# A planner that sets the order of every instruction: transfers booked as one queue of at most eight, hand-over times by pair of engines, and one store for each converted piece

## The chip, the cores and the metric

One core of a Trainium2 chip runs the whole program. The metric is device time in microseconds (us) of one execution. Engines are named as in the profile: PE (matmuls; PEld its weight loads), DVE (VectorE), ACT (ScalarE), POOL (GpSimd) and SP (SyncE, which here issues almost all transfers).

## The reference, cut to what matters

Three layers follow each other; all of it is in 32-bit floats. B, S, D = 4, 448, 64, with 12 heads and a model width of 768.

```python
q_n, k_n = rmsnorm(q, g_q), rmsnorm(k, g_k)
attn = softmax(q_n @ k_n.T / sqrt(64)); x = attn @ v          # heads side by side: 4 x 448 x 768
h = relu(x @ w_in); u, v = h[..., :512], h[..., 512:]         # layer 2
v_s = w_spatial @ layernorm(v) + b_spatial
x = (u * v_s) @ w_out
u = x + (relu(x.T @ w_tok1) @ w_tok2).T                       # layer 3
out = u + relu(u @ w_ch1) @ w_ch2
```

## The kernel before

**Work and stages.** Attention goes by 24 pairs of heads. For a pair, `tp<-ident,raw` are transposes of the scaled q and k on PE, `sc` the scores, `e` the exponentials on ACT, `tp<-ident,e` their transposes, `et` the copies of these, `av` the product with v. Layer 2 (`vps`, `ups`, `sps`, `xps`) runs between the pairs, a batch behind. Then come the token mixing (`h1ps`, `u_ps`) and the channel mixing: `h2ps` (up) and `o_ps` (down), each as seven products of half-size blocks, whose block sums DVE and POOL make (`ut<-ut`, `c<-c,c`, `src<-src`).

**Precision.** Most products take operands split into a high and a low part, three passes each. The split of an operand (`op`, `w`, `wpart`, `xp`, `qt`) is a copy on ACT into the high part and a subtraction on DVE or POOL into the low part. Where inputs are 64-bit, a weight goes through a conversion of one ACT and four DVE instructions (`word`, `wpart`, from `raw`), and the result goes back to DRAM (`c_d`, `wu_d`, `wo_d`, `w_d`) until its stage.

**Shapes of the array.** `sc` contracts over 64 rows, so two heads use the two halves of the array (`64*112`); `av` writes 64 columns and uses it in halves the other way (`128*64`); all other products and the transposes use the whole array. The planner charges `SWITCH` = 200 ns where the kind changes, and prefers to stay in a kind (`NEAR`).

**What sets the order.** The kernel's text only records operations. `Plan.add` gives each a cost on its engine and a lateness (`estimate`), `hop` the time from an operation's end to the start of one that depends on it, and `Plan.place` runs through time and takes, on each engine, the ready operation with the best rank; `issue` does this forwards and backwards eight times and writes the instructions out in the order of the best pass. On the chip each engine takes its instructions strictly in that order, so an instruction that waits holds up all behind it on its engine. `port` is the planner's rule that DVE and POOL don't work from SBUF at the same time with certain operations. A transfer was booked as an occupation of SP of `max(475, size/260)` ns and a lateness of `2400 + 1.2e-3*size` ns. The hop from ACT to PE was 142 + 100 ns, from DVE to PE 128 + 100 ns.

**Lines.** Nearly every instruction is issued by one line (L424 in the profile; the same line is L446 in the changed kernel), so rows are told apart by their tiles.

Of the kernel before, what the change touches and what calls it, by code (L numbers as in the profile page):

```python
# [12 lines left out]
F32 = mybir.dt.float32  # L13
# [8 lines left out]
HI, LO = 0, 1  # L22
# [106 lines left out]
class Banks:  # L129
# [3 lines left out]
    OWN = {"sc": 4, "tp": 2, "mm": 2}  # L133
# [10 lines left out]


class Op:
    __slots__ = ("engine", "call", "cost", "late", "deps", "more", "parts", "port", "dma")


class Plan:  # L150
# [8 lines left out]
    def add(self, engine, fn, args, kwargs):  # L159
        op = Op()  # L160
        op.engine, op.more, op.dma = engine, [], fn == "dma_start"
        op.call = (fn, args, kwargs)
        named = dict(kwargs)
        out = named.pop("out", None)
        rest = list(args)
        if out is None:
            out = rest.pop(0)
        outs = [x for x in (out, named.pop("accum_out", None)) if isinstance(x, Part)]
        ins = [x for x in rest + list(named.values()) if isinstance(x, Part)]
        op.cost, op.late = self.estimate(engine, fn, out, ins, kwargs)  # L170

        sbuf = [x for x in ins if not x.tile.psum]
        op.port = engine == "gpsimd" and bool(sbuf) or engine == "vector" and (
            len(sbuf) > 1 and free(sbuf[1].shape) > 1
            or len(ins) == len(sbuf) and fn in ("tensor_scalar", "tensor_copy"))

        op.parts = 0
        if engine == "tensor" and fn == "matmul":
            op.parts = 1 if ins[0].shape[0] <= 64 else 2 if out.shape[0] <= 64 else 0
        if self.joined:  # L180
            self.joined[0].more.append(op)
            self.joined[0].cost += op.cost
            op = self.joined[0]
        else:
            op.deps = set()
            self.ops.append(op)
        if self.joined is not None:
            self.joined.append(op)
        for x in ins:
            t = x.tile  # L190
            assert t.writers, "read before it is written"
            assert t.make or covered(x, t.writers), "read before all of it is written"
            op.deps.update(w for y, w in t.writers if x.meets(y))
            if t.psum:
                op.deps.update(r for _, r in t.readers if r.engine != engine)
            t.readers.append((x, op))
            t.users.append(op)
        for x in outs:
            t = x.tile
            before = [w for y, w in t.writers if x.meets(y)]  # L200
            if not before:
                self.later.append((op, t.after))
            op.deps.update(before)
            op.deps.update(r for y, r in t.readers if x.meets(y))
            t.writers = [(y, w) for y, w in t.writers if not x.covers(y)] + [(x, op)]
            t.readers = [(y, r) for y, r in t.readers if not x.covers(y)]
            t.users.append(op)
        op.deps.discard(op)
# [8 lines left out]
    def estimate(self, engine, fn, out, ins, kwargs):  # L217

        shape = max((tuple(x.shape) for x in [out] + ins if isinstance(x, Part)), key=free)
        n = free(shape)  # L220
        psum = any(x.tile.psum for x in ins)
        if fn == "dma_start" and engine != "sync":
            size = shape[0] * n * 4
            return 500, 2400 + 5e-3 * size
        if engine == "tensor":
            if fn == "transpose":
                return ins[0].shape[0] / 1.2 + 3, 200
            n = free(ins[1].shape)
            if ins[1].dtype == F32R:
                return 0.223 * n if ins[0].shape[0] <= 64 else n / 2.4 + 15, 200  # L230
            return 0.838 * n if min(ins[0].shape[0], out.shape[0]) <= 64 else n / 0.6, 200
        if engine == "scalar":
            extra = any(isinstance(kwargs.get(k), Part) for k in ("bias", "scale"))
            extra += kwargs.get("accum_out") is not None
            return 0.833 * n + (51 if psum else 94) + 93 * extra, 142
        if engine == "vector":
            if n <= 64:
                return 160, 128
            if fn in ("tensor_scalar", "tensor_copy") and not psum:
                return 0.53 * n + 90, 128  # L240
            pointer = fn == "scalar_tensor_tensor" and any(free(x.shape) == 1 for x in ins)
            return 1.042 * n + 70 + 61 * pointer, 175 if free(out.shape) < n else 128
        if engine == "gpsimd":
            if fn == "tensor_scalar":
                return max(165, 1.3 * n + 35), 75
            pace = 2.0 if any(x.steps and x.steps[-1][0] == "to_broadcast" for x in ins) else 2.4
            return max(165, pace * n + 20), 75
        size = shape[0] * n * 4
        return max(475, size / 260), 2400 + 1.2e-3 * size
# [10 lines left out]
    @staticmethod  # L260
    def hop(a, b):

        if a.engine == b.engine and not a.dma:
            return OWN[a.engine]
        return a.late + TO[b.engine]

    def place(self, before, after, lag, weight, tiles=None):

        ops = self.ops
        left = [len(x) for x in before]  # L270
        ready = [0.0] * len(ops)
        engines = sorted({op.engine for op in ops})
        due = {e: [] for e in engines}
        waiting = {e: [] for e in engines}
        free_at = dict.fromkeys(engines, 0.0)
        start = [0.0] * len(ops)
        parts, port = 0, 0.0
        bank = {}
        if tiles is not None:
            opens, closes, users = tiles  # L280
# [8 lines left out]
        while placed < len(ops):  # L289
# [8 lines left out]
            if e == "tensor" and ops[i].parts != parts:  # L298
# [4 lines left out]
                if near:  # L303
                    x = min(near)
# [5 lines left out]
            if ops[i].port and port <= t and other in due and free_at[other] <= t:  # L310

                free_at[other] = t
                while due[other] and due[other][0][0] <= t:
                    x = heapq.heappop(due[other])[1]
                    heapq.heappush(waiting[other], (weight[x], x))
                if waiting[other] and waiting[other][0][0] < weight[i] and ops[waiting[other][0][1]].port:
                    heapq.heappush(waiting[e], (weight[i], i))
                    e = other
                    i = heapq.heappop(waiting[e])[1]
            if ops[i].port:  # L320
                if port > t:
                    heapq.heappush(due[e], (port, i))
                    continue
                port = t + ops[i].cost
            if tiles is not None and i in opens:
                ks = opens[i]
                kind = ks[0].psum
# [17 lines left out]
            if e == "tensor":  # L345
                end += SWITCH * (ops[i].parts != parts)
                parts = ops[i].parts
            free_at[e] = end
            for s, hop in zip(after[i], lag[i]):
                ready[s] = max(ready[s], end + hop)  # L350
                left[s] -= 1
                if not left[s]:
                    heapq.heappush(due[ops[s].engine], (ready[s], s))
# [75 lines left out]


SWITCH, NEAR = 200, 2500
SHARED = {"vector": "gpsimd", "gpsimd": "vector"}


# [21 lines left out]
def free(shape):  # L456
    n = 1
    for x in shape[1:]:
        n *= x
    return n  # L460
# [11 lines left out]
def attention_moe_mixer(  # L472
# [468 lines left out]
    def prepare_uo(mp):  # L941

        def piece(src, dims, dst):
            raw = weights(mp, "wraw", 2, src, P, dims)
            t = mp.tile([P, 2, NX], F32R, tag="wpart", bufs=2, name="wpart")
            convert(mp, None, 0, raw, P, NX, t[:, HI], t[:, LO], at=t[:, LO].bitcast(U32))
            t = t.bitcast(F32)
            for a in (HI, LO):
                x = t[:, a]
                nc.sync.dma_start(  # L950
                    out=dst[:, a].bitcast(F32),
                    in_=x.rearrange("p (a b) -> p a b", a=dims[0]) if len(dims) > 1 else x)

        n = NX // P
        for i in range(KU):
            for j in range(0, KD, n):
                piece(
                    wdram(w_in)[j * P:(j + n) * P, i * P * W:(i + 1) * P * W].rearrange(
                        "(j p) f -> p j f", p=P), (n, P), wu_d[i][:, :, j:j + n])
                yield  # L960
        for n in range(XN):
            for i in range(KU):
                piece(wdram(w_out)[i * P:(i + 1) * P, n * NX * W:(n + 1) * NX * W], (NX,), wo_d[n][:, :, i])
                yield

    def prepare_next(mp):


        def piece(src, rows, dims, dst):
# [5 lines left out]
            convert(  # L975
                mp, None, 0, raw, rows, n, t[:rows, HI, :n], t[:rows, LO, :n], at=t[:rows, LO, :n].bitcast(U32))
            t = t.bitcast(F32)
            for a in (HI, LO):
                x = t[:rows, a, :n]
                nc.sync.dma_start(  # L980
                    out=dst[:rows, a].bitcast(F32),
                    in_=x.rearrange("p (a b) -> p a b", a=dims[0]) if len(dims) > 1 else x)

        for c, (t, m) in enumerate(TOK):
            piece(wdram(w_tok1)[t:t + m, :], m, (DT,), w1_d[:, :, c])
# [502 lines left out]
```

## Time and profile before

| | before |
|---|---|
| median of three runs | 893.71 us (893.05 to 894.37) |
| profiled execution | 891.53 us |
| its span, first to last instruction | 889.4 us |
| PE busy | 869.6 us (98%) |
| DVE, ACT, POOL busy | 685.6, 537.0, 421.3 us |
| granted TensorE clock, mean over the span | 0.995 |

The profiled execution is 2.1 us longer than its span, and 2.2 us shorter than the median of the runs. A busy PE is not PE at its peak: a matmul that starts late for the array's sake counts as busy.

### The profile page before, as it was taken

Reading aid. Unit: us, or ns where it says so; the run is one execution under the profiler, and the core shown is the slowest. Engines: PE = TensorE matmul, PEld = TensorE weight load, DVE = VectorE, ACT = ScalarE, POOL = GpSimd, SP = SyncE. Lnnn points to the kernel's source line nnn. Section 1 sums busy time; section 2 is a strip of 40 time slices with the busy share of each in tenths; the row PEclk is TensorE's granted clock in tenths of the full one; section 3 lists DMA queues with packets and bytes.
Section 4 is the critical chain, followed back from the end, with each engine's and each line's share of the span. In section 5 each row is a group of like instructions: output and inputs, shape, how many; then the busy total and the mean of one; then the engine's idle time right before and its main releaser. Section 6 shows DMA issues by size and latency. Waiting matters only on the chain.

```text
span 889.4 us, 15926 instructions
## 1 busy us (share of the span) xinstructions
PE 869.6 (98%) x5186; PEld 721.3 (81%) x5186; DVE 685.6 (77%) x1333; ACT 537.0 (60%) x1292; POOL 421.3 (47%) x541
## 2 busy tenths in 40 slices
PE   8998999999999999999999999999999999999998
PEld 5454567678777787777889999999889999999998
DVE  6789898787868667886576357989889886988973
ACT  5998888787877767766544346656225654343331
POOL 3565746776666733664235214154224107524560
PEclk9999999999999999999999999999999999999999
DMA  6545555767545575246588568776554745751441
GB/s 151 160 121 170 166 154 162 199 181 225 134 132 166 148 212 165 50 135 190 189 273 254 172 199 276 235 245 203 172 160 134 231 124 153 222 177 54 143 151 63
DMA packets 149106, 152.30 MB, mean 171 GB/s; under 512 B 77856, under 2 KB 130656, under 8 KB 147488
## 3 DMA queue, kind: packets, MB, share of 16 engines
q1 hardware_dynamic: 148064, 151.06, 57.3%
q8 instruction: 41, 0.67, 0.3%
q14 instruction: 41, 0.34, 0.1%
q10 hardware_dynamic: 960, 0.23, 0.1%
HBM read 112.44 MB, written 38.80 MB: 170 GB/s over the span
## 4 chain that ended last, share of the span: by engine, by line
PE 76%; DVE 8%; ACT 8%; DMA 4%; issue 2%; POOL 1%; SPq 1%; ACTq 0%; DVEq 0%; POOLq 0%
PE o_ps L424 15%; PE h2ps L424 13%; PE tp L424 9%; PE av L424 7%; PE ups L424 6%; PE vps L424 5%; PE sc L424 5%; PE xps L424 5%; PE sps L424 4%; PE u_ps L424 3%; PE h1ps L424 3%; ACT e L424 3%; DVE word L424 2%; DVE c L424 1%; DVE w L424 1%
## 5 line engine op out<-in xcount | busy, mean ns | idle before, releaser
L424 PE MATMUL h2ps<-op,w 128*128 128x448 f32 x756 | 155.4, 367 | 2.4 <-DVE c L424 2.3
L424 PE MATMUL o_ps<-w,op 128*128 128x384 f32 x882 | 153.5, 334 | 1.0 <-DVE u L424 1.0
L424 PEld LDWEIGHTS o_ps<-w,op 128*128 128x128 f32 x882 | 152.8, 188 | 1.6 <-issue 1.6
L424 PEld LDWEIGHTS h2ps<-op,w 128*128 128x128 f32 x756 | 141.2, 188 | 15.3 <-DVE c L424 4.2
L424 ACT ACTIVATE e<-sc,nm 112x448 f32<-112x448 f32 x192 | 122.5, 654 | 23.9 <-DVE nm L424 23.5
L424 DVE TENSOR_REDUCE nm<-sc 112x1 f32<-112x448 f32 x192 | 110.1, 615 | 18.5 <-PE sc L424 18.2
L424 POOL TENSOR_TENSOR src<-src 128x384 f32<-128x384 f32 x48 | 65.8, 1381 | 68.6 <-DMA src<-c_d 50.0
L424 PEld LDWEIGHTS tp<-ident,e 112*128 112x128 f32 x672 | 71.7, 140 | 31.0 <-ACT et L424 9.4
L424 POOL TENSOR_SCALAR e<-e,sums 112x448 f32<-112x448 f32 x112 | 73.4, 673 | 45.9 <-DVE sums L424 33.1
L424 PE MATMUL tp<-ident,e 112*128 112x112 f32 x672 | 89.1, 262 | 4.2 <-ACT et L424 1.7
L424 ACT ACTIVATE op<-c 128x768 fp32r<-128x768 f32 x49 | 41.5, 847 | 84.6 <-PE o_ps L424 81.0
L424 ACT ACTIVATE et<-tp 128x448 f32<-128x448 f32 x144 | 71.4, 528 | 15.7 <-PE tp L424 14.5
L424 DVE SCALAR_TENSOR_TENSOR word<-raw,word 128x256 uint32<-128x256 uint32 (+2 forms) x132 | 72.8, 556 | 1.6
L424 POOL TENSOR_TENSOR u<-u,o 128x384 f32<-128x384 f32 x28 | 40.2, 1453 | 70.4 <-ACT o L424 39.3
L424 DVE TENSOR_SCALAR word<-word 128x256 uint32<-128x256 uint32 (+5 forms) x132 | 55.4, 424 | 20.4 <-ACT word L424 19.3
L424 PE MATMUL ups<-xp,wu 128*128 128x448 f32 x288 | 68.1, 375 | 0.0
L424 DVE TENSOR_TENSOR op<-c,op 128x768 fp32r<-128x768 f32 x49 | 58.2, 1187 | 10.3 <-ACT op L424 10.3
L424 PE MATMUL av<-et,v 128*64 128x448 f32 x288 | 62.9, 563 | 0.0
L424 PE MATMUL xps<-wo,g 128*128 128x256 f32 x432 | 59.9, 288 | 0.0
L424 DVE TENSOR_TENSOR c<-c,h2ps 128x448 f32<-128x448 f32 x84 | 50.1, 616 | 12.6 <-PE h2ps L424 12.5
L424 PE MATMUL vps<-wv,xp 128*128 128x512 f32 x216 | 59.6, 409 | 0.0
L424 PEld LDWEIGHTS ups<-xp,wu 128*128 128x128 f32 x288 | 52.3, 188 | 5.9 <-ACT e L424 0.7
(141 smaller groups left out, 1669.8 us busy)
## 6 DMA issues: line engine op xcount, KB each, us to landing
src<-c_d SPq DMA_DIRECT2D x132, 192.0 KB, 3.1
wu<-wu_d SPq DMA_DIRECT2D x16, 768.0 KB, 4.7
wo<-wo_d SPq DMA_DIRECT2D x12, 1024.0 KB, 6.2
raw<-in_moe_w_ch_dram SPq DMA_DIRECT2D x36, 256.0 KB, 3.4
raw<-in_moe_w_ch_dram SPq DMA_DIRECT2D x24, 384.0 KB, 3.6
raw<-in_q_dram SPq DMA_DIRECT2D x48, 112.0 KB, 3.0
u<-u_d SPq DMA_DIRECT2D x28, 192.0 KB, 3.6
out_dram<-u SPq DMA_DIRECT2D x28, 192.0 KB, 2.2
```

Of the source, the lines that this page charges most:

```text
L424: getattr(getattr(self.nc, op.engine), fn)(*args, **kwargs)
```

## The change

Transfers get a model of their own: each moves for `size/390` ns (or `size/270` for long rows) plus 300 ns of slack, one after the other in one queue, no sooner than 1870 ns (a load) or 1340 ns (a store) after its issue; SP is occupied for 450 ns; and no ninth transfer is issued while eight are under way. Hand-overs between engines come from a table by pair of engines (`LAG`), `HOLD` lets the next user of the shared port start 60 or 110 ns before the booked end, and POOL's broadcast copy (`wide`) is booked at 1.1 instead of 2.0 ns an element. A converted piece (`wpart`) is stored in one transfer of both parts, so that 32 of the program's transfers go.

```diff
+        if op.dma:
+            shape = max((tuple(x.shape) for x in outs + ins), key=free)
+            size, row = 4 * shape[0] * free(shape), 4 * free(shape)
+            store = not (outs and outs[0].tile.make)
+            own = max(173, 3.5e-3 * size) if shape[-1] == 64 else size / (390 if row <= 4096 else 270)
+            op.move = own + 300, 1340 if store else 1870
+            op.cost = ISSUE
+            op.late = sum(op.move) - ISSUE
...
+            if fn == "tensor_copy" and ins[0].steps and ins[0].steps[-1][0] == "to_broadcast":
+                return 1.1 * n, 75
...
-        if a.engine == b.engine and not a.dma:
-            return OWN[a.engine]
-        return a.late + TO[b.engine]
+        if a.dma or a.engine == "fence" or b.engine == "fence":
+            return a.late + TO[b.engine]
+        return OWN[a.engine] if a.engine == b.engine else LAG[a.engine, b.engine]
...
+            if ops[i].dma and tiles is not None and len(landed) >= LANES and landed[-LANES] > t:
+                heapq.heappush(due[e], (landed[-LANES], i))
+                continue
             if ops[i].port:
...
-                port = t + ops[i].cost
+                port = t + ops[i].cost - HOLD[e]
...
+            if ops[i].dma and tiles is not None:
+                own, least = ops[i].move
+                moved = max(t + least, moved) + own
+                landed.append(moved)
+                more = moved - end - ops[i].late
...
+ISSUE, LANES = 450, 8
+HOLD = {"vector": 60, "gpsimd": 110}
+LAG = {
+    ("gpsimd", "scalar"): 88, ("gpsimd", "sync"): 120, ("gpsimd", "vector"): 96, ("gpsimd", "tensor"): 130,
+    ("scalar", "gpsimd"): 188, ("scalar", "sync"): 146, ("scalar", "tensor"): 165, ("scalar", "vector"): 147,
+    ("tensor", "scalar"): 197, ("tensor", "vector"): 198, ("tensor", "sync"): 195, ("tensor", "gpsimd"): 230,
+    ("vector", "gpsimd"): 165, ("vector", "scalar"): 110, ("vector", "sync"): 110, ("vector", "tensor"): 128,
+}
...
-            for a in (HI, LO):
-                x = t[:, a]
-                nc.sync.dma_start(
-                    out=dst[:, a].bitcast(F32),
-                    in_=x.rearrange("p (a b) -> p a b", a=dims[0]) if len(dims) > 1 else x)
+            nc.sync.dma_start(
+                out=dst.bitcast(F32),
+                in_=t.rearrange("p w (a b) -> p w a b", a=dims[0]) if len(dims) > 1 else t)
```

Every engine's order is made anew, so rows differ almost everywhere. Between two pairs of heads the amount of work stays nearly the same; what moves is the order within. Over the whole program PE goes 520 times from one sort of product to another in the order before and 465 times in the new one; 168 of these before, and 144 now, change the shape in which the array is used. Three places:

PE, near the end of the attention (scores of the 23rd pair, values of the pair before it). Before, `sc` and `av` are interrupted by a transpose and a product of layer 2, and the second visit to `sc` is short:

```order
L424 MATMUL sc<-kt,qt 112x448 x12
L424 MATMUL av<-et,v_5410 64x448 x2
L424 MATMUL tp<-ident,raw 128x112
L424 MATMUL sps<-ws,vn 128x448
L424 MATMUL sc<-kt,qt 112x448 x6
L424 MATMUL av<-et,v_5410 64x448 x4
L424 MATMUL av<-et,vrest 64x448 x2
L424 MATMUL ups<-xp,wu 128x448 x2
```

The same place now:

```order
L446 MATMUL sps<-ws,vn 128x448
L446 MATMUL sc<-kt,qt 112x448 x12
L446 MATMUL av<-et,v_5397 64x448 x6
L446 MATMUL av<-et,vrest 64x448 x2
L446 MATMUL sc<-kt,qt 112x448 x12
L446 MATMUL ups<-xp,wu 128x448 x6
```

The scores and values stand in one block, and the half-array work is left once where it was left twice.

ACT, at the start of the program (`whole` with `gg` is the first pair's k, `word` the first weight's conversion, `ry` the second pair's norms). Before:

```order
L424 ACTIVATE sq<-raw 112x512
L424 ACTIVATE ry<-ra 112x16
L424 ACTIVATE ry<-ry 112x16
L424 ACTIVATE word<-raw 128x512
L424 ACTIVATE whole<-tp,gg 128x448
L424 ACTIVATE word<-raw 128x512
L424 ACTIVATE e,sums<-sc,nm 112x448 x4
```

And now:

```order
L446 ACTIVATE sq<-raw 112x512 x2
L446 ACTIVATE whole<-tp,gg 128x448
L446 ACTIVATE word<-raw 128x512
L446 ACTIVATE ry<-ra 112x16
L446 ACTIVATE ry<-ry 112x16
L446 ACTIVATE e,sums<-sc,nm 112x448 x4
```

`whole` has moved ahead of `word`, and `ry` behind it; the second `word` comes later.

DVE, in the up products, where the third product's sums begin (`c<-c,h2ps` empties a bank of PSUM, `word` are conversions of `w_ch2`). Before:

```order
L424 TENSOR_TENSOR op<-ut,op 128x1344
L424 TENSOR_TENSOR c_8586<-c_7976,h2ps 128x448 x2
L424 TENSOR_SCALAR word<-word 128x384 x3
L424 TENSOR_TENSOR c_8586<-c_7976,h2ps 128x448
L424 SCALAR_TENSOR_TENSOR word<-raw,word 128x384
L424 TENSOR_SCALAR word<-word 128x384
L424 SCALAR_TENSOR_TENSOR word<-raw,word 128x384
L424 TENSOR_TENSOR c_8586<-c_7976,h2ps 128x448
```

And now:

```order
L446 TENSOR_TENSOR op<-ut,op 128x1344
L446 TENSOR_TENSOR c_8581<-c_8001,h2ps 128x448 x2
L446 TENSOR_SCALAR word<-word 128x384
L446 TENSOR_TENSOR c_8581<-c_8001,h2ps 128x448
L446 TENSOR_SCALAR word<-word 128x384
L446 TENSOR_TENSOR c_8581<-c_8001,h2ps 128x448
L446 SCALAR_TENSOR_TENSOR word<-raw,word 128x384
L446 TENSOR_SCALAR word<-word 128x384
L446 TENSOR_TENSOR c_8581<-c_8001,h2ps 128x448
```

The three conversions that stood in a row between two sums stand singly now.

## Rows read from the trace of the kernel before

**Rows 1.** The page's first lines: busy time, share, instructions.

```profile
span 889.4 us, 15926 instructions
PE 869.6 (98%) x5186; PEld 721.3 (81%) x5186; DVE 685.6 (77%) x1333; ACT 537.0 (60%) x1292; POOL 421.3 (47%) x541
```

**Rows 2.** Stretches of the span: length; busy PE, PEld, DVE, ACT, POOL; clock; DMA share; GB/s.

```profile
25.00:75.00 50.00, 48.88 (x300) 25.10 (x300) 42.11 (x92) 49.97 (x144) 28.96 (x51) 1.00 0.56 152
...
115.00:435.00 320.00, 316.95 (x2089) 238.66 (x2086) 246.76 (x596) 236.16 (x654) 198.15 (x306) 1.00 0.56 160
...
575.00:731.00 156.00, 153.61 (x756) 140.66 (x755) 136.50 (x211) 75.28 (x130) 47.64 (x36) 1.00 0.62 184
```

**Rows 3.** What PE's idle time waited for: total us, times, longest.

```profile
PE tp L424 <- ACT et L424: 2.4, 6, 0.6
PE h2ps L424 <- DVE c L424: 2.3, 3, 1.0
PE sc L424 <- ACT whole L424: 2.2, 1, 2.2
...
PE o_ps L424 <- DVE u L424: 1.0, 2, 0.6
...
PE tp L424 <- POOL e L424: 0.2, 1, 0.2
```

**Rows 4.** PE in order of time around one visit to `sc`: start, us.

```profile
207.74 0.55 PE L424 MATMUL tp<-ident,e 112*128 112x112 f32 x4
208.21 1.48 PE L424 MATMUL sc<-kt,qt 64*112 64x448 f32 x12
209.62 1.44 PE L424 MATMUL xps<-wo,g 128*128 128x256 f32 x10
210.90 0.45 PE L424 MATMUL tp<-ident,e 112*128 112x112 f32 x3
```

**Rows 5.** PE around a visit with half as many `sc`.

```profile
125.48 0.88 PE L424 MATMUL sc<-kt,qt 64*112 64x448 f32 x6
126.29 0.50 PE L424 MATMUL vps<-wv,xp 128*128 128x512 f32 x1
```

**Rows 6.** The chain that ended last: long runs of one product without a pause (start, us).

```profile
47.63 2.26 PE tp L424 x22
...
500.55 5.73 PE xps L424 x48
```

**Rows 7.** The start, in order of time: ACT, PE, and POOL's scaling of the second pair.

```profile
11.18 0.21 ACT L424 ACTIVATE ry<-ra 112x16 f32<-112x16 f32 x1 [2.26 <-POOL ra L424]
...
12.73 0.66 ACT L424 ACTIVATE word<-raw 128x512 f32<-128x512 f32 x1 [1.09 <-DMA raw<-in_moe_w_in_dram]
12.91 2.22 POOL L424 TENSOR_TENSOR raw<-raw,ry 112x512 f32<-112x512 f32 x2
13.30 0.62 ACT L424 ACTIVATE whole<-tp,gg 128x448 f32<-128x448 f32 x1
13.97 3.13 PE L424 MATMUL sc<-whole 64*112 64x448 f32 x8 [2.23 <-ACT whole L424]
```

**Rows 8.** DVE and PE in order of time, in the up products.

```profile
645.93 3.04 DVE L424 TENSOR_SCALAR word<-word 128x384 f32<-128x384 f32 x3
...
649.55 2.11 PE L424 MATMUL h2ps<-op,w 128*128 128x448 f32 x9 [0.55 <-DVE c L424]
```

**Rows 9.** ACT and PE behind one late store, in order of time.

```profile
340.92 0.43 ACT L424 ACTIVATE word<-raw 128x256 f32<-128x256 f32 x1 [1.43 <-DMA c_d<-word]
...
342.99 0.60 PE L424 MATMUL tp<-ident,raw 112*128 112x112 f32 x4 [1.09 <-DVE et L424]
```

**Rows 10.** The tile `word`: idle time until its stores landed, and their time to landing.

```profile
  DMA c_d<-word: 14.7, 8
...
DMA to landing us min/median/max: 1.8/3.6/8.1
```

**Rows 11.** SP in order of time: the issue of one store of half a piece.

```profile
72.53 0.45 SPq L424 DMA_DIRECT2D wu_d<-wpart  x1
```

More of the change, by code (lines that the diff above doesn't have):

```diff
@@ L146 @@
 class Op:
-    __slots__ = ("engine", "call", "cost", "late", "deps", "more", "parts", "port", "dma")
+    __slots__ = ("engine", "call", "cost", "late", "deps", "more", "parts", "port", "dma", "move")
 class Plan:
@@ L170, in add @@
         op.cost, op.late = self.estimate(engine, fn, out, ins, kwargs)
+        op.move = None
+        if op.dma:
[6 more added lines that the diff above has]
+            op.late = sum(op.move) - ISSUE
         sbuf = [x for x in ins if not x.tile.psum]
@@ L277, in place @@
         parts, port = 0, 0.0
+        landed, moved = [], 0.0
         bank = {}
@@ L319, in place @@
                     i = heapq.heappop(waiting[e])[1]
+            if ops[i].port and port > t:
+                heapq.heappush(due[e], (port, i))
+                continue
+            if ops[i].dma and tiles is not None and len(landed) >= LANES and landed[-LANES] > t:
+                heapq.heappush(due[e], (landed[-LANES], i))
+                continue
             if ops[i].port:
-                if port > t:
-                    heapq.heappush(due[e], (port, i))
-                    continue
-                port = t + ops[i].cost
+                port = t + ops[i].cost - HOLD[e]
             if tiles is not None and i in opens:
@@ L348, in place @@
             free_at[e] = end
+            more = 0.0
+            if ops[i].dma and tiles is not None:
[3 more added lines that the diff above has]
+                more = moved - end - ops[i].late
             for s, hop in zip(after[i], lag[i]):
-                ready[s] = max(ready[s], end + hop)
+                ready[s] = max(ready[s], end + hop + more)
                 left[s] -= 1
@@ L977, in piece @@
             t = t.bitcast(F32)
[L978 to L982, printed above, removed]
+            assert len(dims) == 1
+            nc.sync.dma_start(out=dst[:rows].bitcast(F32), in_=t[:rows, :, :n])
         for c, (t, m) in enumerate(TOK):
```

## The prediction

> **What bounds the kernel now.** I read the page's first lines, then the table by stretches, then the waits of PE, then PE's own order of time. The page [rows 1] says that PE is busy for 869.6 of 889.4 us: only 19.8 us of the span are idle on the busiest engine. The table by stretches [rows 2] says where another engine is full as well: from 25 to 75 us ACT is busy for 49.97 of 50 us, so there a PE that gets faster soon waits for ACT; from 115 to 435 us PE has 316.95 of 320 us and ACT 236.16; in the up products (575 to 731 us) PE has 153.61 of 156 us and DVE 136.50, close behind. PE's waits [rows 3] are thirteen rows that add up to 15.4 us, in pieces of 0.2 to 2.2 us: the start (2.2, PE waits for `whole`), the emptying of banks by DVE in the up and down products (2.3 and 1.0), and small ones in the attention.
>
> So a new order can gain in two places: in those waits, and inside PE's busy time, where the array is changed from one shape to another.
>
> **The price of a change of shape.** In [rows 4] PE goes from transposes (207.74) to twelve `sc` matmuls and on to ten `xps`, and reaches the next transposes at 210.90: 3.16 us. The work in that: a transpose costs 2.26 / 22 = 0.103 us and an `xps` 5.73 / 48 = 0.119 us where they run without a pause [rows 6]; two `sc` (one pair of heads on two halves) cost 0.20 us, since six more matmuls make a visit longer by (209.62 - 208.21) - (126.29 - 125.48) = 0.60 us [rows 4, 5]. That is 4 x 0.103 + 6 x 0.20 + 10 x 0.119 = 2.80 us. The other 0.36 us are the two changes of shape: **0.18 us each**. It is no wait, the rows show no idle time there.
>
> **The change, part by part.**
>
> *The order on PE.* The order before has 168 changes of shape, the new one 144: at the 23rd pair `sc` and `av`, cut up before, stand in one block. 24 x 0.18 = 4.3 us. Twelve of the 24 lie in the first eight pairs, where ACT is full; there I count half (bounds nothing and all), the other twelve in full: 2.2 + 1.1 = **3.3 us less**, bounds 2.2 and 4.3. The 31 other alternations that go don't change the shape; I count nothing for them.
>
> *The start.* Now ACT takes `word` first, which waits for a weight's transfer until 12.73, and `whole`, which PE needs, starts at 13.30; PE stands idle for 2.23 us until 13.97 [rows 7]. With `whole` first it can start as soon as the transposes are done, 2.23 us before 13.97, that is at 11.74; 0.62 us for itself and 0.05 us to PE (13.30 + 0.62 to 13.97) let `sc` begin at 12.4, 1.5 us sooner. But `ry`, on which POOL's scaling of the second pair hangs, stood at 11.18, 1.73 us before that scaling's start at 12.91; now it comes behind `word`, which ends at 13.39, so that the scaling starts at about 13.39 + 1.73 = 15.1, 2.2 us later. A third chunk of scores, now ahead of the second pair's transposes on PE, fills some of that. I take half of the gain, **0.7 us less**; bounds 1.5 less and 1.5 more.
>
> *Conversions no longer in a row.* DVE's three `word` instructions took 3.04 us in one piece and PE then waited 0.55 us for a bank [rows 8]; the five waits of this sort are 2.3 + 1.0 us [rows 3]. In the new order the three stand singly between sums. A late store is the other case: a `c_d` store landed late, ACT idled 1.43 us before `word`, DVE's part of the conversion came later for it, and `et`, next on DVE, kept PE waiting 1.09 us [rows 9]. A book that lets transfers queue behind each other puts such a conversion later. Together 4.4 us; other places can come to wait, so I take half, **2.2 us less**; bounds nothing and 4.4.
>
> *Shorter hand-overs.* By the kernel's own formula `whole` occupies ACT for 0.833 x 448 + 51 + 93 = 517 ns, so ACT was free at 13.82 and PE began 0.15 us later [rows 7]. The old book had 0.242 us for this hop, the new one has 0.165 us: the new one is right here. It takes away slack with which PE's order stood up to late inputs. The waits not named above (15.4 - 2.2 - 3.3 - 1.1 = 8.8 us, 1.5 of them before the first matmul) could shrink or grow by it; I count nothing, bounds 7 us either way.
>
> *Stores of pieces in one transfer.* 32 transfers go, 0.45 us of SP each [rows 11]: 14 us of a queue that issues and waits in 889 us, none of it in PE's waits [rows 3]. What hides it is that the pieces are read back several pairs later. If that cover were gone, a reader would wait for the low part's subtraction, which stood right behind the first store on SP before as well; I count nothing, bounds 0.5 us either way.
>
> *Shorter lateness for transfers.* The new book lets a lone 128 KB store land 131072 / 390 + 300 + 1340 = 1.98 us after its issue, the old one 0.50 + 2.56 = 3.06 us. The trace has 1.8 at least and 3.6 in the median for the stores of `word` [rows 10]: right for a free queue, 1.6 us short for the usual one, unless the booked queue makes up for it. The book also lets a store land sooner than a load. A rule speaks against that: the Trainium skill, "DMA: Bandwidth & Descriptors", section "Anatomy of one DMA — SWDGE (gpsimd) path", states (for the path of GpSimd, which these stores don't take) a fixed cost of some 2.0 us, mostly the target's receipt and longest where the target is HBM, and an addition of bytes / 436e9 s; an estimate from that page is 2.3 us for a 128 KB store, 0.3 us more than booked, and by it this part would lose up to 0.3 us for a conversion that waits, and nothing where ACT has room. The trace's minimum of 1.8 us is on the book's side; its median is above both.
>
> **Sum.** 3.3 + 0.7 + 2.2 = 6.2 us less. For the profiled execution: 891.5 - 6.2 = 885.3 us, with a span near 883. The median of the runs shown is 2.2 us above the profiled execution, so **893.7 - 6.2 = 887.5 us**.
>
> **Rivals.**
>
> *Nothing moves* (893.7, give or take 1.8 us; 0.2% is about what a measurement of this kernel can tell from no change). What PE saves it gives back as waits for ACT before 75 us and for DVE after 575 us, both nearly full [rows 2]. For it: ACT's 49.97 of 50 us. Against it: in 115 to 435 us ACT has a quarter of its time free, and half of the saved changes of shape lie beyond the first eight pairs.
>
> *Slower: stores booked too short.* ACT's `word` is placed when its buffer should be back; the store is later, ACT stands, and everything behind it on ACT too. Before, ACT waits so 8 times, 14.7 us in all [rows 10], and the one in [rows 9] cost PE 1.09 us. With 1.1 us for each that reaches PE, it decides from 6 more of them on, which eat the 6.2 us, and from 8 the kernel is slower by more than 1.8 us. At ten it is 893.7 + 11 - 6.2 = 898.5 us. For it: 3.6 against 1.98 us. Against it: the booked queue adds what stands ahead.
>
> *Nearly all waits go too.* All five bank waits and the late store (4.4), all changes of shape (4.3), the start (1.5), and half of the small waits (3.5): 13.7 us, 880 us. For it: the hop that the rows bear out. Against it: the trace's own durations vary under an order that is fixed.
>
> **How the numbers follow.** Forecast 0.60, with a range of its own from 883.5 to 891.5 us; nothing moves 0.15; slower 0.15; nearly all waits 0.10. Faster by over 0.2%: 0.60 + 0.10 = 0.70; within 0.2%: 0.15; slower: 0.15. A range from 881.5 to 896 us holds the forecast, the case of no change and half of the last: 0.80.
>
> **What would show each step.** In the new profile the same stretch of PE rows should still show 0.18 us for a change of shape, and PE's busy time should be lower by 3 to 4 us; if it is as before, the first step is wrong. The first `sc` should begin near 12.4 us. PE's waits for `c<-c,h2ps` and `u<-u,o_ps` should be below 3.3 us in all. ACT's wait for `c_d<-word` well above 14.7 us, with PE waiting behind it, would show the slower rival. The prediction fails most easily at the waits of the attention, which I set to no change and which no row of before can tell for an order that is new throughout.

## The result, and the profile after

The changed kernel takes 899.93 us (median of 6 runs, 898.22 to 902.67) beside 893.18 us (6 runs, 890.62 to 894.37) of the kernel before: ratio 1.0081, 95% interval 1.0062 to 1.0101. It is slower; the forecast was 887.5 us. Its profiled execution took 901.0 us with a span of 898.9 us.

First the page of the changed kernel: span, busy time, and the chain that ended last, by engine; the last line is the chain of the kernel before.

```profile
span 898.9 us, 15854 instructions
PE 866.1 (96%) x5186; PEld 720.2 (80%) x5186; DVE 713.1 (79%) x1333; ACT 539.3 (60%) x1292; POOL 416.7 (46%) x541
...
PE 60%; DVE 17%; DMA 9%; ACT 8%; issue 3%; POOL 1%; SPq 1%; ACTq 0%; DVEq 0%; POOLq 0%
```

```profile
PE 76%; DVE 8%; ACT 8%; DMA 4%; issue 2%; POOL 1%; SPq 1%; ACTq 0%; DVEq 0%; POOLq 0%
```

Beside [rows 1] PE's busy time fell by 3.5 us, and its idle time (span less busy) rose from 19.8 to 32.8 us. DVE does the same 1333 instructions in 27.5 us more, and its share of the chain doubled. The share of DMA doubled too, but that is this kernel's own: in the four other kernels below that give the port free early behind POOL it is 3 to 5%, and DVE's 11 to 13%. So PE's busy time did get a little shorter, DVE is slower, and PE stands longer.

Next the table by stretches (columns as in [rows 2]), and PE's waits, the five costliest and the smallest.

```profile
0.00:25.00 25.00, 18.22 (x106) 13.01 (x106) 12.45 (x25) 13.78 (x35) 6.37 (x25) 0.93 0.59 145
25.00:75.00 50.00, 45.01 (x276) 23.05 (x278) 44.67 (x96) 49.68 (x139) 31.12 (x49) 1.00 0.57 162
...
115.00:435.00 320.00, 316.07 (x2090) 239.56 (x2087) 263.52 (x609) 239.33 (x658) 200.98 (x311) 1.00 0.55 160
...
575.00:731.00 156.00, 152.31 (x749) 137.71 (x748) 127.79 (x201) 74.33 (x129) 38.54 (x33) 1.00 0.59 174
```

```profile
PE tp L446 <- ACT et L446: 4.5, 7, 1.0
PE sc L446 <- ACT e L446: 3.8, 3, 2.5
PE h2ps L446 <- DVE c L446: 3.2, 6, 1.0
PE xps L446 <- DMA wo<-wo_d: 2.1, 1, 2.1
PE o_ps L446 <- DVE u L446: 1.9, 2, 1.6
...
PE tp L446 <- PE sc L446: 0.2, 1, 0.2
```

The view has 21 rows that add up to 28.8 us, where [rows 3] are thirteen with 15.4 us. No single new wait explains the loss: they are many, of 0.2 to 2.5 us. Summed over the view by what ended them, those for DVE went from 5.8 to 8.2 us, those for ACT from 7.0 to 15.4. So a slower DVE reaches PE at most in part by direct waits; how the rest of its time gets there is followed in single places below, and not in sum. From 115 to 435 us DVE is busy for 16.8 us more than in [rows 2], for 13 more instructions.

The last `h1ps` (the end of the token mixing) tells where the loss had come by then; the view is the tile `h1ps` of the changed kernel (duration in ns, least, median and most; then first and last start in us).

```profile
L446 PE MATMUL h1ps<-xh,w x176: 331/334/441, 466.0 to 572.3; 128*128 128x384 f32 x176
```

Before it was at 567.2, so 5.1 us are lost up to there. The other 4.4 us of the spans' difference of 9.5 us are lost behind it, where the up and down products stand.

**Where DVE's time went.** In the changed kernel, DVE and POOL in order of time, at a sum over 128 x 1 elements.

```profile
263.53 2.04 POOL L446 TENSOR_TENSOR raw<-raw,ry 112x512 f32<-112x512 f32 x2
263.58 1.00 DVE L446 TENSOR_TENSOR lrz<-lry 128x1 f32<-128x1 f32 x1 [0.82 <-ACT lry L446]
264.51 0.49 DVE L446 COPY et<-tp 128x336 f32<-128x336 f32 x1
264.93 0.66 DVE L446 TENSOR_TENSOR lrz<-lrz,lra 128x1 f32<-128x1 f32 x1
```

And these operations over the whole kernel, from the views of the tiles `lrz` and `et`.

```profile
L446 DVE TENSOR_TENSOR lrz<-lry x16: 150/160/1308, 118.4 to 473.9; 128x1 f32<-128x1 f32 x16
...
L446 DVE COPY et<-tp x48: 458/504/509, 25.8 to 437.5; 128x336 f32<-128x336 f32 x48
```

The first of them in the kernel before:

```profile
L424 DVE TENSOR_TENSOR lrz<-lry x16: 144/162/1586, 118.1 to 473.3; 128x1 f32<-128x1 f32 x16
```

`lrz` needs 0.16 us, and took 1.00 us: from POOL's start to the end of the first of its two operations. The second one took 0.66 us and ended at 265.59, where POOL's pair ended (263.53 + 2.04 = 265.57). The copy between them, which reads a bank and no tile of SBUF, ran beside POOL in its usual time. The Trainium skill, "Trainium Architecture — The Big Picture", section "What this means for kernel authors", calls the port pair that DVE and GpSimd share an exclusive lock and not a split of bandwidth; the rows agree: the instruction isn't slowed in proportion, it ends 0.02 us behind POOL's operation, and it counts as busy meanwhile.

I counted DVE instructions that took over 0.2 us more than the lower quartile of their kind in the kernel before: 113 there, 68.7 us over in sum; 142 in the changed kernel, 93.9 us over. The 25.2 us between them are nearly all of DVE's 27.5. Of the 142, 141 started while a POOL operation was running. The sums over one element show what such a wait is, but not the loss: the planner's rule for the port asks for a second operand of more than one element, so `HOLD` doesn't touch them, and 12 of them were long before and 8 are now. The extra stands in the operations that the rule covers: 101 long ones before, 134 now.

The longest one stood behind three POOL operations in a row; the next view is that place in order of time, with what waited.

```profile
542.06 1.40 POOL L446 TENSOR_TENSOR x<-two,x 64x384 f32<-64x384 f32 x1 [0.29 <-ACT two L446]
542.51 4.14 DVE L446 SCALAR_TENSOR_TENSOR word<-raw,word 128x384 uint32<-128x384 uint32 x1
...
543.42 1.84 POOL L446 TENSOR_TENSOR xh<-x,xh 128x768 fp32r<-128x768 f32 x1
545.23 2.29 POOL L446 TENSOR_TENSOR src<-src 128x384 f32<-128x384 f32 x2
546.57 0.54 DVE L446 TENSOR_TENSOR x<-u_ps,x 64x384 f32<-64x384 f32 x1
547.04 1.30 DVE L446 TENSOR_TENSOR xh<-x,xh 128x768 fp32r<-128x768 f32 x1
...
548.39 0.79 PE L446 MATMUL h1ps<-xh,w 128*128 128x384 f32 x3 [0.61 <-DVE xh L446]
```

This `word` usually takes 0.55 us; behind it on DVE stood `x`, then `xh`, for which PE waited. In the down products `op`, 0.95 us where it runs alone, took 1.77 us beside a `src`; PE's longest wait there is for `u`, which comes next on DVE:

```profile
775.17 1.38 POOL L446 TENSOR_TENSOR src<-src 128x384 f32<-128x384 f32 x1 [0.78 <-DMA src<-c_d]
775.60 1.77 DVE L446 TENSOR_TENSOR op<-c,op 128x768 fp32r<-128x768 f32 x1
...
777.29 0.54 DVE L446 TENSOR_TENSOR u<-u,o_ps 128x384 f32<-128x384 f32 x1
...
777.98 1.30 PE L446 MATMUL o_ps<-w,op 128*128 128x384 f32 x6 [1.59 <-DVE u L446]
```

### The profile page after: what moved, and what is told of

Read it like the earlier page. It is cut to its first block, busy times and chain, and to the rows that moved or that the text cites. A ratio compares the mean times of both kernels' runs of the same rounds, so it can differ in the third digit from the quotient of the medians.

```text
span 898.9 us, 15854 instructions
## 1 busy us (share of the span) xinstructions
PE 866.1 (96%) x5186; PEld 720.2 (80%) x5186; DVE 713.1 (79%) x1333; ACT 539.3 (60%) x1292; POOL 416.7 (46%) x541
## 4 chain that ended last, share of the span: by engine, by line
PE 60%; DVE 17%; DMA 9%; ACT 8%; issue 3%; POOL 1%; SPq 1%; ACTq 0%; DVEq 0%; POOLq 0%
PE h2ps L446 10%; PE o_ps L446 9%; PE tp L446 7%; PE av L446 7%; PE xps L446 6%; PE sc L446 5%; PE vps L446 5%; PE ups L446 5%; DVE op L446 3%; DVE c L446 3%; DVE word L446 3%; ACT e L446 3%; PE sps L446 3%; DVE w L446 3%; DMA c_d<-word 2%
## 5 line engine op out<-in xcount | busy, mean ns | idle before, releaser
L446 PE MATMUL h2ps<-op,w 128*128 128x448 f32 x756 | 157.2, 367 | 3.7 <-DVE c L446 3.2
L446 ACT ACTIVATE e<-sc,nm 112x448 f32<-112x448 f32 x192 | 122.4, 650 | 26.5 <-DVE nm L446 26.3
L446 POOL TENSOR_TENSOR src<-src 128x384 f32<-128x384 f32 x48 | 60.4, 1265 | 87.3 <-DMA src<-c_d 76.9
L446 POOL TENSOR_SCALAR e<-e,sums 112x448 f32<-112x448 f32 x112 | 76.6, 700 | 46.0 <-DVE sums L446 25.8
L446 DVE SCALAR_TENSOR_TENSOR word<-raw,word 128x256 uint32<-128x256 uint32 (+2 forms) x132 | 82.3, 624 | 2.0
L446 DVE TENSOR_SCALAR word<-word 128x256 f32<-128x256 f32 (+5 forms) x132 | 59.5, 453 | 19.5 <-ACT word L446 18.3
L446 POOL TENSOR_TENSOR u<-u,o 128x384 f32<-128x384 f32 x28 | 38.3, 1386 | 67.0 <-ACT o L446 36.9
L446 DVE TENSOR_TENSOR op<-c,op 128x768 fp32r<-128x768 f32 x49 | 62.7, 1280 | 5.4 <-ACT op L446 5.1
L446 PE MATMUL av<-et,v 128*64 128x448 f32 x288 | 60.7, 550 | 1.4 <-ACT et L446 1.4
L446 PE MATMUL xps<-wo,g 128*128 128x256 f32 x432 | 58.1, 287 | 2.1 <-DMA wo<-wo_d 2.1
L446 PEld LDWEIGHTS xps<-wo,g 128*128 128x128 f32 x432 | 53.8, 191 | 3.9 <-issue 3.5
```

Source lines behind the costliest of these rows:

```text
L446: getattr(getattr(self.nc, op.engine), fn)(*args, **kwargs)
```

## The experiments

The planner's booked times are called the book here. Four theories were set against each other. **Theory 1**: the shorter hand-overs took away slack. **Theory 2**: the booked transfers put conversions where their stores aren't back. **Theory 3**: any new order draws its waits by chance. **Theory 4**: `HOLD`, which gives the shared port to the next user before the booked end, lets DVE's instructions meet POOL's. Every kernel plans an order of its own, so each ratio holds its edit and one draw of an order.

### Each part alone, on the kernel before

b_lag: the hand-overs alone.

```diff
-        if a.engine == b.engine and not a.dma:
-            return OWN[a.engine]
-        return a.late + TO[b.engine]
+        if a.dma or a.engine == "fence" or b.engine == "fence":
+            return a.late + TO[b.engine]
+        return OWN[a.engine] if a.engine == b.engine else LAG[a.engine, b.engine]
```

> The kernel before with the table of hand-over times alone. If the shorter hand-overs cost the time (theory 1: less slack, so PE meets late inputs), the ratio to before is 1.005 to 1.010 and PE's waits for ACT and DVE rise from 15.4 us to 22 us or more, while its busy time falls by 3 us or so. If the booking of transfers costs it (theory 2), the ratio is 0.995 to 1.002. If any new order draws its waits anew by chance (theory 3), the ratio lies anywhere from 0.994 to 1.010 and says nothing of the other parts.

b_dma: the model of the transfers alone (`op.move`, `landed`, `moved`).

```diff
+            if ops[i].dma and tiles is not None and len(landed) >= LANES and landed[-LANES] > t:
+                heapq.heappush(due[e], (landed[-LANES], i))
+                continue
...
-                ready[s] = max(ready[s], end + hop)
+                ready[s] = max(ready[s], end + hop + more)
```

> The kernel before with the booking of transfers alone (one queue, at most eight under way, 300 ns of slack, 450 ns of SP). Theory 2 (transfers booked too early): ratio 1.005 to 1.010, and the waits of ACT, POOL and PE that end with a transfer rise. Theory 1: ratio 0.995 to 1.002. Theory 3: anywhere from 0.994 to 1.010.

b_store: one store for a converted piece, alone.

```diff
-            for a in (HI, LO):
-                x = t[:, a]
-                nc.sync.dma_start(
...
+            nc.sync.dma_start(
+                out=dst.bitcast(F32),
```

> The kernel before with the 32 pairs of stores of converted pieces made into one transfer each, and nothing else. Theories 1 and 2: ratio 0.998 to 1.002, since no work on PE's path goes. Theory 3: this edit too makes a new order, so the ratio can be off by 0.3% or more either way.

b_port: the port and the cost of POOL's wide copy; b_hold and b_wide, below, take this pair apart.

```diff
+            if fn == "tensor_copy" and ins[0].steps and ins[0].steps[-1][0] == "to_broadcast":
+                return 1.1 * n, 75
...
-                port = t + ops[i].cost
+                port = t + ops[i].cost - HOLD[e]
```

> The kernel before with the shared port's book let go 60 or 110 ns sooner and POOL's broadcast copy booked at 1.1 ns an element. Theories 1 and 2: ratio 0.998 to 1.002. If the port's book is what costs (theory 4), DVE's busy time rises from 685.6 to 705 us or more and the ratio is above 1.003. Theory 3: off by 0.3% or more either way.

Measured, with the other single parts (busy times and waits from each kernel's one profile):

| kernel | ratio, 95% interval | PE busy | DVE busy | PE's waits |
|---|---|---|---|---|
| b_lag | 1.0018 (0.9996 to 1.0040) | 868.5 | 683.6 | 20.9 |
| b_dma | 1.0032 (1.0012 to 1.0051) | 868.0 | 683.4 | 19.2 |
| b_store | 0.9988 (0.9969 to 1.0007) | 867.2 | 685.0 | 18.2 |
| b_port | 1.0078 (1.0052 to 1.0104) | 866.8 | 716.3 | 21.7 |
| b_hold | 1.0043 (1.0028 to 1.0058) | 869.0 | 711.8 | 21.8 |
| b_wide | 0.9964 (0.9951 to 0.9978) | 868.7 | 681.5 | 14.8 |

Of these only the two kernels with the early release have DVE at 711.8 us or more, and the pair with it costs as much as the whole change. b_dma is slower too, by less than theory 2 gave, and its interval overlaps that of b_hold.

### The port, taken out and turned round

b_hold is the early release alone on the kernel before; b_wide is the cost of the wide copy alone; a_nohold is the changed kernel without the release; a_margin is the changed kernel with the same times added as a margin.

```diff
 a_nohold
-                port = t + ops[i].cost - HOLD[e]
+                port = t + ops[i].cost
 a_margin
-                port = t + ops[i].cost - HOLD[e]
+                port = t + ops[i].cost + HOLD[e]
```

> The kernel before with the early release of the port alone, without the new cost of the broadcast copy. Theory 4: DVE's busy time of 705 us or more and a ratio of 1.004 to 1.010. If the copy's cost is what counted in the run of both, DVE is near 685 us and the ratio 0.998 to 1.003.

> The kernel before with the new cost of POOL's broadcast copy alone. Theory 4: DVE's busy time near 685 us and a ratio of 0.997 to 1.003. If the copy's cost is the cause: ratio 1.004 to 1.010.

> The changed kernel, with the shared port booked until the end of the operation again (HOLD not subtracted), all else as changed. Theory 4 (the early release lets POOL's operation reach the port before DVE's, and DVE then stands for the rest of it): DVE's busy time falls from 713.1 us to 690 us or less, and the ratio to before is 0.994 to 1.002. Theories 1 and 2 (hand-overs, transfers): DVE's busy time may fall, but the ratio stays above 1.004. Theory 3 (any new order draws its waits by chance): ratio anywhere from 0.994 to 1.010.

> The changed kernel, with 60 and 110 ns added to the port's booked time where the change subtracts them. Theory 4: DVE's busy time at or below that of the run without subtraction, 670 to 690 us, and a ratio of 0.990 to 1.002, the loss being a matter of the margin. Other theories: no tie between the margin and DVE's busy time.

a_nohold: ratio 0.9998 (0.9984 to 1.0012). The whole loss is gone, DVE is back at 684.9 us, and PE's busy time is 861.3 us, 8.3 below [rows 1].

a_margin: ratio 1.0336 (1.0319 to 1.0352), 920.86 us, the slowest of all, though DVE's busy time fell to 674.8 us. Theory 4 was right on DVE's time and wrong on the ratio, for which it gave 0.990 to 1.002. The profile, ACT and then PE in order of time, shows another cause for 12.1 us of it:

```profile
538.74 0.43 ACT L446 ACTIVATE word<-raw 128x256 f32<-128x256 f32 x1 [2.54 <-DMA c_d<-word]
541.45 0.43 ACT L446 ACTIVATE word<-raw 128x256 f32<-128x256 f32 x1 [2.27 <-DMA c_d<-word]
545.26 0.86 ACT L446 ACTIVATE two<-u_ps 64x384 f32<-64x384 f32 x2 [3.39 <-DMA c_d<-word]
```

```profile
547.45 0.69 PE L446 MATMUL tp<-ident,x 128*128 128x128 f32 x2 [12.12 <-DVE x L446]
```

Two conversions in a row on ACT and then `two` itself each stood until a `c_d` store had landed, and on `two` hang `x` and PE's next transposes: 12.1 us in one wait. That is the price of a late store at the worst place. The changed kernel has no such wait (its longest is 2.54 us), so this doesn't speak against the early release as the cause there. But it shows that an order can lose 3.4% without any early release, and that a margin isn't the cure by itself.

### Which side of the port, and how far

```diff
 a_holdg
-HOLD = {"vector": 60, "gpsimd": 110}
+HOLD = {"vector": 0, "gpsimd": 110}
 a_holdv
-HOLD = {"vector": 60, "gpsimd": 110}
+HOLD = {"vector": 60, "gpsimd": 0}
 a_hold220
-HOLD = {"vector": 60, "gpsimd": 110}
+HOLD = {"vector": 0, "gpsimd": 220}
```

> The changed kernel, with the shared port given free early only while GpSimd holds it (110 ns), not while VectorE does. Theory 4 (VectorE's instruction is started beside the rest of a GpSimd operation and is lengthened by it): VectorE's busy time stays near that of the changed kernel, above 700 us (713.1 there, 684.9 without the early release), and the time stays slower than before, ratio 1.003 to 1.010. If it is the other direction (60 ns while VectorE holds it) that costs: VectorE's busy time near 685 us and a ratio of 0.998 to 1.002. Theory 3 (any new order): VectorE's busy time says nothing about the ratio.

> The changed kernel, with the port given free early only while VectorE holds it (60 ns). Theory 4: VectorE's busy time is near 685 us, GpSimd's goes up instead, if anything does, and the ratio is 0.997 to 1.003. If this direction costs: VectorE's busy time over 700 us, ratio 1.003 to 1.010. If it takes both directions together, both of these kernels stay below 700 us.

> The changed kernel, with the port given free 220 ns early while GpSimd holds it, and not early while VectorE does. Without it VectorE was busy for 684.9 us (ratio 0.9998), at 110 ns for 701.5 us (1.0113). Theory 4 (VectorE's instruction, sent beside the rest of a GpSimd operation, waits for its end): the cost grows, VectorE's busy time 710 to 725 us, ratio above 1.011. If the 110 ns only drew an unlucky order (theory 3): no relation, VectorE's busy time near 700 us or below and a ratio anywhere in 1.000 to 1.012.

a_holdg: 1.0113 (1.0093 to 1.0133); a_holdv: 1.0006 (0.9992 to 1.0020). Their pages, a_holdg's and then a_holdv's:

```profile
span 900.0 us, 15857 instructions
PE 867.4 (96%) x5186; PEld 722.1 (80%) x5186; DVE 701.5 (78%) x1333; ACT 539.5 (60%) x1292; POOL 422.3 (47%) x541
```

```profile
span 891.7 us, 15853 instructions
PE 869.0 (97%) x5186; PEld 720.9 (81%) x5186; DVE 682.9 (77%) x1333; ACT 536.3 (60%) x1292; POOL 407.9 (46%) x541
```

It is the direction in which DVE may follow POOL early, as theory 4 had it, and by more than its range (1.003 to 1.010); the other direction costs nothing that can be measured. In a_holdg the longest wait of PE leads back to one DVE instruction; in order of time:

```profile
62.18 0.73 POOL L446 TENSOR_TENSOR wpart<-wpart 128x256 fp32r<-128x256 f32 x1
62.60 3.09 DVE L446 SCALAR_TENSOR_TENSOR wpart<-raw,wpart 128x256 uint32<-128x256 uint32 x1
...
63.05 1.27 POOL L446 TENSOR_TENSOR wv<-word,wv 128x512 fp32r<-128x512 f32 x1
64.29 1.12 POOL L446 TENSOR_TENSOR xp<-over,xp 128x448 fp32r<-128x448 f32 x1
65.38 0.37 POOL L446 TENSOR_SCALAR rz<-rz 112x16 f32<-112x16 f32 x1
...
65.72 0.42 ACT L446 ACTIVATE wpart<-wpart 128x256 fp32r<-128x256 f32 x1 [2.21 <-DVE wpart L446]
...
67.85 0.64 PE L446 MATMUL tp<-ident,wide 112*128 112x112 f32 x4 [3.79 <-ACT et L446]
```

DVE's `wpart`, 0.42 us where it runs alone, stood behind POOL's operations one after the other, ACT behind DVE, and ACT's `et` came late for PE, which waited for 3.79 us.

a_hold220: 1.0126 (1.0103 to 1.0148). The ratio is in the range that theory 4 gave, but not above a_holdg's by more than the intervals, and DVE's busy time is 700.4 us, where theory 4 expected 710 to 725. A cost that grows with the size of the release is not shown.

### Orders drawn by edits with no meaning

```diff
 c_act1
-            return 0.833 * n + (51 if psum else 94) + 93 * extra, 142
+            return 0.833 * n + (52 if psum else 95) + 93 * extra, 142
 c_dve1
-            return 1.042 * n + 70 + 61 * pointer, 175 if free(out.shape) < n else 128
+            return 1.042 * n + 71 + 61 * pointer, 175 if free(out.shape) < n else 128
```

> The kernel before, with 1 ns added to the planner's cost of a ScalarE operation: a change with no meaning, which only draws a new order (158 changes of array shape on TensorE instead of 168). Theory 3 (a new order draws its waits by chance): the time moves by 0.2% or more to either side although nothing was changed, VectorE's busy time stays at 681 to 686 us, TensorE's falls by 10 x 0.18 = 1.8 us, and its waits leave 15.4 us by some us. Theories 1, 2 and 4 (a cost of the change itself): ratio within 0.998 and 1.002.

> The kernel before, with 1 ns added to the planner's cost of a VectorE operation: a second order drawn by an edit with no meaning (170 changes of array shape instead of 168). Theory 3: the time moves by 0.2% or more to either side, TensorE's busy time stays within 1 us of 869.6, its waits leave 15.4 us. Theories 1, 2 and 4: ratio within 0.998 and 1.002. Together with the other one it gives the size of what an order alone does, to which the parts of the change are held.

c_act1: 1.0006 (0.9986 to 1.0027), DVE busy for 678.5 us, PE's waits 16.6 us. c_dve1: 1.0007 (0.9986 to 1.0029), 684.1 and 18.4 us. A new order alone didn't make up 0.8% in either, nor the 0.2% that theory 3 gave, nor DVE's 713 us. Two draws are few: a_margin shows that the size of what an order can cost isn't bounded by them.

### The parts without the port, put together

b_ws has the wide copy's cost and the stores in one transfer, as in the diffs above, on the kernel before; b_lws adds the hand-overs, b_dws the booked transfers.

> The kernel before with two parts of the change alone: the cost of the wide copy on GpSimd and the stores in one transfer. Alone they gave 0.9964 and 0.9988. If parts add up: 0.995 (0.993 to 0.997), 887 us beside a kernel before of 891 us, and the best of all kernels here. If an order is drawn anew each time (theory 3), whose size two edits with no meaning showed as 0.0006 and 0.0007: anywhere within 0.996 to 1.001.

> The same two parts and the shorter hand-overs (ratio 1.0018 alone); no booked transfers, no early release of the port. If parts add up: 0.997 (0.995 to 0.999). Theory 1 (shorter hand-overs are what gives back TensorE's saved time): TensorE's busy time falls to 861 to 866 us as it did without the early release (861.3), and its waits rise to 20 us or more; the ratio is above that of the kernel without hand-overs by 0.002 or more.

> The same two parts and the booked transfers (ratio 1.0032 alone); old hand-overs, no early release of the port. If parts add up: 0.998 (0.996 to 1.000). Theory 2 (the booked transfers give it back): TensorE's waits rise to 19 us or more (19.2 with the booked transfers alone), ScalarE's wait for a store of a converted weight stands above 14.7 us, and the ratio is above that of the kernel without booked transfers by 0.002 or more. If neither this one nor that with the hand-overs is slower than the one with neither, the loss lies in no single part.

b_ws: 1.0005 (0.9993 to 1.0017); b_lws: 1.0003 (0.9988 to 1.0018); b_dws: 1.0002 (0.9982 to 1.0022). Parts don't add up: b_ws was to be the best and isn't. So ratios from 0.9964 to 1.0032, which is what the eleven kernels without POOL's early release span (a_margin aside), can't be read as the worth of a part; neither theory 1 nor theory 2 is borne out. b_wide, at 0.9964, is faster than the kernel before and the changed one, but b_ws, which has its edit too, is not.

All five kernels with POOL's early release lie above those eleven: 1.0043 to 1.0126 (the lowest, b_hold, and the highest of the eleven, b_dma, have intervals that overlap), DVE busy for 700.4 to 716.3 us against 678.5 to 691.4. DVE's long instructions, counted as above, part them as well, and a_margin falls with the eleven: among the operations that the port's rule covers there are 117 to 136 long ones in the five and 79 to 107 in all others, the kernel before with them; of the sums over one element, which the rule doesn't cover, 6 to 14 and 6 to 12. Within the five, more time on DVE doesn't mean a greater loss: b_hold has 711.8 us and 1.0043, a_holdg 701.5 and 1.0113. Which of DVE's waits reach PE differs from order to order.

## Why the prediction was wrong

**The step that failed** is the part by part costing: the release of the port (`HOLD`) has no term in it at all, though it is in the change as described. The prediction took every duration as it stood in the trace of before, DVE's too, and looked for changes in the order and in waits alone. But DVE's durations hold its waits for POOL, and a row that the prediction used shows it. The three `word` of [rows 8] are read there as 3.04 us of DVE's work; one of them takes 0.35 us where it runs alone, and POOL was at work throughout:

```profile
643.61 7.50 POOL L424 TENSOR_TENSOR w<-src,w 128x384 fp32r<-128x384 f32 x6 [11.27 <-PE h2ps L424]
```

So some 2 of the 3.04 us were waits for the port. The term that should have stood in the sum is that of a_nohold against the changed kernel: 1.0081 / 0.9998, some 0.8% or 7.4 us. Other pairs of kernels that differ in POOL's release give it as 0.4% (b_hold against before) to 1.3% (a_hold220 against a_nohold).

That term isn't all of the miss: 887.5 + 7.4 = 894.9 us, and 899.9 were measured. The 6.2 us that the sum takes off didn't come either, since a_nohold, with everything of the change but the release, gives 0.9998 and not 0.993. Of its three terms none is shown (below); why a_nohold gains nothing stays open.

The early release is shown as the cause of the loss (it costs when added to the kernel before, the loss goes when it is taken out, and one direction alone does it). How 110 ns in the book become waits for whole operations on the chip is only argued: an instruction that is sent while POOL works waits for the end, and where POOL's next operation stands ready it can miss that turn too, as at 542.51. There is a second way, which no run tells from this one: for the last 110 ns of an operation POOL is still booked, so in the plan the port goes to DVE's next operation whatever the ranks, and the release changes whose turn it is as well.

**Shapes of the array (-3.3 us).** The sum agrees with the change in PE's busy time, 869.6 to 866.1 us. I don't take it as shown: a_hold220 has the same 144 changes of shape and 870.1 us, a_nohold 140 and 861.3, b_lag 148 and 868.5. Other delays that count as busy are as large as the term. Whether a change of shape still costs 0.18 us in the new order wasn't read from its rows.

**The start (-0.7 us).** The view is the start of the changed kernel, ACT, POOL and PE in order of time.

```profile
12.00 0.64 ACT L446 ACTIVATE whole<-tp,gg 128x448 f32<-128x448 f32 x1 [0.69 <-DVE gg L446]
...
12.69 1.76 PE L446 MATMUL sc<-whole 64*112 64x448 f32 x8 [0.79 <-ACT whole L446]
...
16.40 2.04 POOL L446 TENSOR_TENSOR raw<-raw,ry 112x512 f32<-112x512 f32 x2
...
16.99 1.01 PE L446 MATMUL sc<-whole 64*112 64x448 f32 x4 [2.54 <-ACT e L446]
```

The first `sc` came at 12.69, where 12.4 was forecast and 13.97 stands in [rows 7]. POOL's scaling came at 16.40, not 15.1, and the third chunk of scores waited 2.54 us for ACT's `e`. At 25 us PE had started 106 matmuls in either kernel: the gain was given back at once, within the term's bounds.

**Conversions no longer in a row (-2.2 us).** Wrong in sign: PE's waits for `c` and `u` are 3.2 + 1.9 = 5.1 us, against 3.3 in [rows 3]. The three `word` do stand apart. The sums `c<-c,h2ps` kept their time (0.61 us, none of the 84 was long), but in places what stands ahead of them on DVE did not: behind the wait of 0.52 us at 639.68 is a `w` of 1.37 instead of 0.55 us, behind that of 1.59 us at 777.98 the `op` and a `w`, each 0.8 us too long. Others have another cause, such as 0.81 us at 648.29 (see the rivals).

**The rest.** Stores in one transfer, set to nothing: 0.9988 alone, its interval takes in 1. Hand-overs, set to nothing within 7 us: 1.0018 alone. Transfers, set to nothing: 1.0032 alone, 1.0002 beside two other parts. The small waits were to stay within 7 us; all waits together rose by 13.4 us.

**The rivals.** The one that was slower gave 898.5 us, close to the time measured, by a mechanism that had little part in it: that the number is near is luck. The view is that of the tile `word` in the changed kernel, as [rows 10].

```profile
  DMA c_d<-word: 22.7, 11
...
DMA to landing us min/median/max: 1.7/4.0/6.9
```

ACT does stand longer for the stores, 22.7 against 14.7 us. In one place at least this reached PE: ACT stood for 5.64 us until 646.30, the conversion on DVE and the sum behind it came later, and PE waited 0.81 us at 648.29. But in a_holdv ACT stands for 26.5 us in 16 waits, with a ratio of 1.0006. The sum of these waits doesn't tell the loss; a single one can cost much where PE's next work hangs on it, as in a_margin. The rival of no change describes a_nohold: PE saves 8.3 us of busy time, its waits rise from 15.4 to 21.1 us, and the timed ratio is 0.9998. Its profiled span is 3.0 us shorter than that of before, but its profiled execution, 888.4 us, is also 2.9 us shorter than the median of its runs, so one profile can't tell what the gain is worth.

## What to carry to other kernels

A trace's duration of a VectorE instruction can hold a wait for GpSimd: before keeping durations fixed under a new order, compare the least with the most of one form, and see whether the long ones started while GpSimd was at work. Any edit that lets the two come closer in time needs a term of its own, sized by whole GpSimd operations (up to three in a row here) and not by the nanoseconds that the book gives away. Where an order is drawn anew by each edit, one kernel for each part says little of the part: here two edits with no meaning moved the time by 0.06 and 0.07%, single parts by -0.36 to +0.32%, and the parts didn't add up. What held was a group of kernels with the part against a group without it.

## What the runs showed of the hardware that was not expected

A VectorE sum of one element in a row, 0.16 us by its median, took up to 1.31 us beside GpSimd (1.59 in the kernel before), and a `word` of 0.55 us took 4.14 us through three GpSimd operations in a row, while copies from PSUM (0.46 to 0.51 us in all 48) never lengthened. In that place and in a_holdg's at 62.60 the waiting instruction had started before GpSimd's next operation and didn't get the next turn.
